# Four parts at once in a spectral-mixing kernel: tables turned by the DMA crossbar, stage-1 evacuations shared anew, a table angle moved, and a drain by groups

## The chip, the cores and the metric

One core of a Trainium2 chip. The metric is the device time in microseconds (us). Most executions of one kernel agree within 0.3%. The kernel before takes 173.03 us (median of 3, 173.02 to 173.04).

The engines carry the profile's names: PE is TensorE (matmuls; PEld its weight loads), DVE is VectorE, ACT is ScalarE, POOL is GpSimd, and SP is SyncE, on whose queue most DMAs are issued. PSUM is the memory into which matmuls write; a result is evacuated when ACT or DVE copies it out. The granted clock is the share of TensorE's full clock that the profile records in a stretch.

## The reference

```python
x = A_x                                            # 1 x 2048 x 512, bf16
W = w_r + 1j * w_i                                 # 2048 x 257
y = irfft2(rfft2(layernorm(x)) * W, s=(2048, 512)).astype(bf16)
h = x + y
r = relu(layernorm(h) @ w1 + b1)                   # 512 -> 1792
out = h + ((r * r) @ w2 + b2)                      # 1792 -> 512
```

The Fourier transform over the 2048 rows is split as 128 x 16, and everything is matmuls with sine and cosine tables. Six stages matter below. Stage 1 transforms along the 128-long axis with a table KF that is folded with LayerNorm's 1/sigma (KFr), and gives Bt. Stage 2 transforms the 512 columns (table GF, result U). Stage 3 finishes the row transform (table EF, results AB and X), and the spectral weights follow on VectorE (mA, mB, Z, M). Stage 4 goes back along the rows (table EI, result T), stage 5 along the columns (table GI, result R), and stage 6 along the other row axis (table KI). LayerNorm and the MLP follow.

## The kernel before

The inverse tables EI and KI are the transposes of EF and KF. The kernel before makes them with TensorE, and copies and negates them on ScalarE and VectorE:

```python
def transposed(o, ks, kf=False):                   # TensorE, into a PSUM tile
    for j, k in enumerate(ks):
        for i in range(2):
            nc.tensor.transpose(o[:, P*(2*j+i):P*(2*j+i)+P], EF[:, k, i, :], ident[:])
    if kf:
        nc.tensor.transpose(o[:, 2*P*len(ks):2*P*len(ks)+P], KF[:, 0:P], ident[:])
def table_i(o, ks):                                # ScalarE
    nc.scalar.copy(EI[:, sl, 0:2, :], o[...])
def table_neg(ks):                                 # VectorE
    nc.vector.tensor_scalar(EI[:, .., 2, :], EI[:, .., 0, :], -1.0, None, ALU.mult)
```

PSUM tiles of the first half come from one pool: four buffers of two banks each. A stage-1 step of two row groups takes one such buffer; a split step takes two, and uses half of each, so that ScalarE empties one and VectorE the other:

```python
ps = tc.alloc_tile_pool(name="ps", bufs=4, space=PSUM)
def mm_tile(name, dt=FP32):
    return ps.tile([P, 4096 // size(dt)], dt, tag="mm", name=name)

def stage1(g0, n=0, split=False, pre=None, cp=nc.scalar.copy):
    if split:
        two = [mm_tile("p1a"), mm_tile("p1b")]
        pts = [pt[:, 0:512] for pt in two]
    else:
        pt = mm_tile("p1"); pts = [pt[:, 0:512], pt[:, 512:1024]]
    ...                                            # 8 matmuls
    if split:
        for t, cph in ((0, nc.scalar.copy), (1, nc.vector.tensor_copy)):
            cph(dst[:, 2*t:2*t+2], pts[t]...)
    else:
        cp(dst, pt[:]...)
...
angles_g(1)                                        # GpSimd: two angle rows, ahead of the power
ln1_rstd(10, 14)                                   # GpSimd: 1/sigma of groups 10 to 13
...
stage1(10, cp=nc.vector.tensor_copy)
# W1, W2, b1, b2 loads issued here
stage1(12)
# GF's last column halved, EF's sines negated (VectorE)
tr08 = stage1(14, split=True, pre=lambda o: transposed(o, (0, 8), True))
```

The drain, between stage 5 and the MLP, with `warm` a run of matmuls on ones whose results nobody reads:

```python
s5(0); s5(1); s5(2, True); s5(3, True)             # stage 5, groups 0 to 3
s5b(0); s5b(1)                                     # R = even + odd, even - odd (VectorE)
s6(0); s6b(0, True); s6(1); s6a(1); s6b(1)         # stage 6, residual, statistics
rstd(0); norm(0)
warm(idle[:], 12)
s5b(2)
transp(0, 0); transp(0, 1)                         # LayerNorm output turned for the MLP
for c in range(5): run(c)                          # the MLP
```

## Time and profile before

The prediction below shows the lines themselves. They boil down to this table, with the starts in us from the start of the span.

| what | before |
|---|---|
| timed median | 173.03 |
| span of the profiled execution | 171.1 |
| busy: PE, VectorE (DVE), ScalarE (ACT) | 92%, 74%, 62% |
| last half of Bt starts on DVE | 19.71 |
| PE's last wait before a stretch without gaps | ends 29.10 |
| stage 5's first matmul | 50.07 |
| MLP's first matmul | 57.13 |

From the MLP's first matmul on nothing changes but for a few copies that the drain now postpones to there, so any gain has to show up in one of the last four rows.

### The profile page before, as it was taken

What the parts mean: (1) busy time and instruction counts of PE and PEld (TensorE: products, weight loads), DVE (VectorE), ACT (ScalarE), POOL (GpSimd) and SP (SyncE); (2) the same over time, 40 slices, a digit from 0 to 9 for tenths busy, and PEclk for the clock granted to TensorE, in tenths of its full rate; (3) what the DMA queues carried; (4) which work ended last, traced back from release to release, by engine and by line L of the source; (5) the groups of instructions that cost most, each with busy time, mean ns of one, the idle gap of its engine ahead of it and who ended that gap; (6) DMA issues with size and microseconds to landing.
All of it is one profiled execution on the core that took longest, in us unless ns stands there. A gap on an engine that the chain in (4) does not pass through costs nothing.

```text
span 171.1 us, 2723 instructions
## 1 busy us (share of the span) xinstructions
PE 158.0 (92%) x982; PEld 93.0 (54%) x997; DVE 125.9 (74%) x294; ACT 106.7 (62%) x188; POOL 36.3 (21%) x63
## 2 busy tenths in 40 slices
PE   3978897999989899899999999999999999999992
PEld 1455665877853675466445444544544454566461
DVE  6998789899957699758997577498667567578321
ACT  3999587998977582288662677254377534478200
POOL 7788800000000002235000135000035200025000
PEclk9999999999999999999999999999999999999999
DMA  5970759910000000010001100001000001010011
GB/s 158 349 261 2 215 168 397 297 35 2 0 0 4 0 0 2 32 35 0 0 21 31 44 0 0 2 31 34 31 31 0 0 31 34 13 48 0 0 59 38
DMA packets 7918, 10.29 MB, mean 60 GB/s; under 512 B 2272, under 2 KB 6368, under 8 KB 7904
## 3 DMA queue, kind: packets, MB, share of 16 engines
q1 hardware_dynamic: 7744, 9.19, 16.6%
q0 software_dynamic: 160, 0.92, 1.8%
q8 instruction: 8, 0.13, 0.3%
q14 instruction: 6, 0.05, 0.1%
HBM read 8.01 MB, written 2.10 MB: 59 GB/s over the span
## 4 chain that ended last, share of the span: by engine, by line
PE 69%; DVE 19%; ACT 6%; issue 3%; POOL 1%; DVEq 0%; POOLq 0%; ACTq 0%
PE ph L688 29%; PE po L721 25%; DVE st L221 4%; PE p L568 3%; PE p L362 3%; PE p L643 2%; ACT U L379 2%; PE po L709 2%; DVE KFr L232 2%; PE p L587 1%; DVE hs L591 1%; DVE mA L437 1%; ACT X L409 1%; DVE mB L437 1%; DVE Z L442 1%
## 5 line engine op out<-in xcount | busy, mean ns | idle before, releaser
L688 PE MATMUL ph<-UT,W 128*128 128x384 bf16 (+2 forms) x278 | 49.8, 336 | 1.5 <-ACT UT L647 1.0
L691 ACT ACTIVATE rl<-ph,b1f 128x384 bf16<-128x384 f32 (+2 forms) x70 | 41.5, 602 | 14.2 <-PE ph L688 11.0
L721 PE MATMUL po<-W,act 128*128 128x512 bf16 x203 | 48.1, 379 | 0.4
L692 DVE TENSOR_TENSOR act<-rl 128x384 bf16<-128x384 bf16 (+2 forms) x70 | 34.2, 514 | 16.2 <-ACT rl L691 15.7
L695 POOL TENSOR_TENSOR hb<-hs,b2b 128x512 f32<-128x512 bf16 x16 | 18.4, 1151 | 102.6 <-DVE act L692 102.6
L688 PEld LDWEIGHTS <-W 128*128 128x128 bf16 x280 | 27.4, 98 | 22.7 <-issue 1.9
L721 PEld LDWEIGHTS <-act 128*128 128x128 bf16 x210 | 20.4, 98 | 21.8
L725 DVE TENSOR_TENSOR ot<-po,hb 128x512 bf16<-128x512 f32 x15 | 10.3, 688 | 9.3 <-PE po L721 8.0
L571 ACT COPY od<-p 128x256 f32<-128x256 f32 x16 | 5.9, 368 | 9.1 <-PE p L568 9.0
L647 ACT COPY UT<-p 128x768 bf16<-128x768 bf16 (+2 forms) x5 | 4.2, 841 | 10.8 <-PE p L643 10.8
L591 DVE SCALAR_TENSOR_TENSOR hs<-p,xs 128x512 bf16<-128x512 f32 x15 | 10.2, 683 | 0.8 <-PE p L587 0.5
L265 PE MATMUL p<-ones 128*128 128x512 bf16 x22 | 7.3, 476 | 2.9 <-POOL ones L152 2.9
L568 PE MATMUL p<-GI,T 128*128 128x256 bf16 x64 | 9.1, 272 | 0.6 <-DVE T L489 0.2
L265 PEld LDWEIGHTS <-ones 128*128 128x128 bf16 x41 | 4.4, 109 | 7.6 <-POOL ones L152 2.9
L602 ACT ACTIVATE junk<-hs 128x512 bf16<-128x512 bf16 x6 | 3.8, 630 | 7.6 <-DVE hs L591 7.6
L362 PE MATMUL p<-GF,Bt 128*128 128x256 bf16 x64 | 8.3, 273 | 0.0
L568 PEld LDWEIGHTS <-T 128*128 128x128 bf16 x64 | 6.2, 97 | 3.9 <-issue 0.9
L250 PE MATMUL p<-KFr,xs 128*128 128x256 bf16 x28 | 6.4, 273 | 2.0 <-DVE KFr L232 2.0
L577 DVE TENSOR_TENSOR R<-p,od 128x256 bf16<-128x256 f32 x16 | 6.6, 414 | 2.1 <-ACT od L571 2.1
L221 DVE BATCH_NORM_STATS2 st<-xs 128x6 f32<-128x512 bf16 x12 | 7.8, 676 | 0.0
L491 ACT CAST T<-p 128x1024 bf16<-128x1024 f32 x7 | 7.2, 1027 | 0.0
L362 PEld LDWEIGHTS <-Bt 128*128 128x128 bf16 x64 | 6.1, 98 | 1.4 <-DVE Bt L257 0.4
(173 smaller groups left out, 228.7 us busy)
## 6 DMA issues: line engine op xcount, KB each, us to landing
W<-in_B_w_dram SPq DMA_DIRECT2D x2, 1792.0 KB, 9.7
out_dram<-ot SPq DMA_DIRECT2D x15, 128.0 KB, 1.8
xs<-in_A_x_dram SPq DMA_DIRECT2D x3, 512.0 KB, 5.6
WB<-in_A_w_r_dram SPq DMA_DIRECT2D x1, 578.2 KB, 5.3
WB<-in_A_w_i_dram SPq DMA_DIRECT2D x1, 578.2 KB, 6.3
xs<-in_A_x_dram SPq DMA_DIRECT2D x2, 256.0 KB, 3.3
b2b<-in_B_b_dram SPq DMA_DIRECT2D x1, 128.0 KB, 8.9
out_dram<-ot SPq DMA_DIRECT2D x2, 64.0 KB, 1.5
```

The source lines that it names most:

```text
L221: nc.vector.bn_stats(st[:], xs[:, g, :])
L265: nc.tensor.matmul(o, lhsT=ones[:, 0:P], rhs=ones[:], start=True, stop=True)
L362: nc.tensor.matmul(puv[:, :, e, :], lhsT=Bt[:, 2 * t + 1 - e, 2 * pr + q, :], rhs=GFv[:, t, :, e, :], start=(t == 0), stop=(t == 1))
L491: nc.scalar.copy(dst, src[0])
L568: nc.tensor.matmul(pe[:, 256 - 256 * e:512 - 256 * e], lhsT=T2[:, lt, g].rearrange("p q s -> p (q s)"), rhs=GI[:, lt, :], start=(r == 0), ...
L591: nc.vector.scalar_tensor_tensor(hs[:, g, :], Ys.pop(g)[:], WSC, xs[:, g, :], ALU.mult, ALU.add)
L688: nc.tensor.matmul(ph[:, 0:n], lhsT=W1[:, d, bass.ts(f, P)], rhs=UT[:, d, 0:n], start=(d == 0), stop=(d == ND - 1))
L691: nc.scalar.activation(rl[:, 0:n], ph[:, 0:n], ACT.Relu, bias=b1f[:, f:f + 1], scale=1.0)
L692: sq = nc.vector.tensor_tensor(act[:, f, 0:n], rl[:, 0:n], rl[:, 0:n], ALU.mult)
L695: add = nc.gpsimd.tensor_tensor(hb[:, g, :], hs[:, g, :], b2b[:], ALU.add)
L721: nc.tensor.matmul(po[:], lhsT=act[:, f, bass.ts(i, P)], rhs=W2[:, f, :], start=(f == 0), stop=(f == NF - 1))
L725: nc.vector.tensor_tensor(ot[:], po[:], hb[:, g, :], ALU.add)
```

## The change

The intent is to take the making of the inverse tables off the three compute engines and give it to the DMA crossbar, to use the room this makes on ScalarE for the stage-1 evacuations, and to shorten the drain by letting group 1's sum and difference come out of matmuls (with a negated table, GIn), so that groups 0 and 1 don't queue on VectorE. The core of the diff, cut:

```diff
-    EF = fwd.tile([P, 9, 3, P], ...)   EI = fwd.tile([P, 9, 3, P], ...)   EN = ...
+    EF = fwd.tile([P, 3, 9, P], ...)   EI = fwd.tile([P, 9, 4, P], ...)
+    GIn = persist.tile([P, 2, 256], BF16, name="GIn")
-    def transposed ... table_i ... table_neg ... first_tables
+    def turned(dst, src):
+        nc.sync.dma_start_transpose(out=dst, in_=...)
@@ stage 1
-    angles_g(1)
-    ln1_rstd(10, 14)
+    nc.gpsimd.tensor_scalar(fiG[:, 512:768], ...)
+    ln1_rstd(10, 14)
+    nc.gpsimd.tensor_scalar(fiG[:, 768:1024], ...)
-    stage1(10, cp=nc.vector.tensor_copy)
-    stage1(12)
+    stage1(10)
+    stage1(12, split=True)
     # GF, EF negation
-    tr08 = stage1(14, split=True, pre=lambda o: transposed(o, (0, 8), True))
+    stage1(14, split=True)
+    turned(EI[:, :, 0, :], EF[:, 0, :, :])         # 9 blocks of sines
+    turned(KI[:].unsqueeze(1), KF[:, 0:P])
+    for k in (0, 8):
+        turned(EI[:, k:k+1, 1, :], EF[:, 1, k, :])
+    turned(EI[:, :, 2, :], EF[:, 2, :, :])         # 9 blocks of negated sines
     ...
+    turned(EI[:, 1:8, 1, :], EF[:, 1, 1:8, :])     # 7 blocks of cosines
+    turned(EI[:, 1:8, 3, :], Cn[:])                # 7 blocks of negated cosines
+    # W1, W2, b1, b2 loads now issued here
@@ spectral part, after pair 5
     sin_of(GI, fiI)
+    nc.scalar.activation(GIn[:], <the even angles of fiI>, ACT.Sin, scale=-SIN_SCALE)
@@ drain
-    s5(0); s5(1); s5(2, True); s5(3, True)
-    s5b(0); s5b(1); s6(0); s6b(0, True); s6(1); s6a(1); s6b(1); rstd(0); norm(0)
-    warm(idle[:], 12)
-    s5b(2); transp(0, 0); transp(0, 1)
+    s5_first(0)        # the odd sum in a bank of its own
+    s5_whole(1)        # 8 matmuls make sum and difference, one ACT copy takes both
+    s5b(0); s6(0); s6(1)
+    rest = [s5(2, True), s5(3, True)]              # their od copies postponed
+    s6a(1); s6b(0, True); s6b(1); ...
+    warm(idle[:], 11)
+    # sqrt, reciprocal, norm, 4 transposes and one copy, group by group
+    for r in rest: r()
+    s5b(2)
```

More of the change, by code (lines that the diff above doesn't have):

```diff
@@ L88 @@
     GF = fwd.tile([P, 2, 512], BF16, name="GF")
-    EF = fwd.tile([P, 9, 3, P], BF16, name="EF")
-    EI = fwd.tile([P, 9, 3, P], BF16, name="EI")
+    EF = fwd.tile([P, 3, 9, P], BF16, name="EF")
+    EI = fwd.tile([P, 9, 4, P], BF16, name="EI")
     ON_PE = (2, 4, 6)
-    Cn = fwd.tile([P, len(ON_PE), P], BF16, name="Cn")
+    Cn = fwd.tile([P, 7, P], BF16, name="Cn")
     NO_M = (5, 6)
-    EN = fwd.tile([P, len(NO_M), 2 * P], BF16, name="EN")
     KFr = fwd.tile([P, G, 256], BF16, name="KFr")
@@ L191 @@
     nc.gpsimd.tensor_scalar(cols[:, 1:2], pF[:, 0:1], 128.0, 16384.0, ALU.mult, ALU.add)
-    def angles_g(t):
-        o = 512 * t
-        for r, q in ((0, QT), (256, HT)):
-            nc.gpsimd.tensor_scalar(fiG[:, o + r:o + r + 256], idxL[:, r:r + 256], cols[:, t:t + 1], float(q),
-                                    ALU.mult, ALU.add)
     def table_e(i):
-        nc.scalar.activation(EF[:, :, i, :], fiE[i][:].bitcast(I16)[:, ::2].rearrange("p (a b) -> p a b", a=9),
+        nc.scalar.activation(EF[:, i, :, :], fiE[i][:].bitcast(I16)[:, ::2].rearrange("p (a b) -> p a b", a=9),
                              ACT.Sin, scale=SIN_SCALE)
@@ L265, in warm @@
             nc.tensor.matmul(o, lhsT=ones[:, 0:P], rhs=ones[:], start=True, stop=True)
-    def transposed(o, ks, kf=False):
-        for j, k in enumerate(ks):
-            for i in range(2):
-                nc.tensor.transpose(o[:, P * (2 * j + i):P * (2 * j + i) + P], EF[:, k, i, :], ident[:])
-        if kf:
-            nc.tensor.transpose(o[:, 2 * P * len(ks):2 * P * len(ks) + P], KF[:, 0:P], ident[:])
-    def table_i(o, ks):
-        n, sl = len(ks), slice(ks[0], ks[-1] + 1, ks[1] - ks[0])
-        nc.scalar.copy(EI[:, sl, 0:2, :], o[:, 0:2 * P * n].rearrange("p (a k b) -> p a k b", a=n, k=2))
-    def table_neg(ks):
-        nc.vector.tensor_scalar(EI[:, ks[0]:ks[-1] + 1, 2, :], EI[:, ks[0]:ks[-1] + 1, 0, :], -1.0, None, ALU.mult)
+    def turned(dst, src):
+        nc.sync.dma_start_transpose(out=dst, in_=src.rearrange("p a b -> p (a b)") if len(src.shape) == 3 else src)
     def angles_c(sl):
@@ L287, in table_c @@
     def table_c(sl):
-        nc.scalar.activation(EF[:, sl, 1, :], fiE[1][:].bitcast(I16)[:, ::2].rearrange("p (a b) -> p a b", a=9)[:, sl],
+        nc.scalar.activation(EF[:, 1, sl, :], fiE[1][:].bitcast(I16)[:, ::2].rearrange("p (a b) -> p a b", a=9)[:, sl],
                              ACT.Sin, scale=SIN_SCALE)
@@ L312 @@
     ln1_fold(6, 10)
-    angles_g(1)
+    nc.gpsimd.tensor_scalar(fiG[:, 512:768], idxL[:, 0:256], cols[:, 1:2], float(QT), ALU.mult, ALU.add)
     ln1_rstd(10, 14)
+    nc.gpsimd.tensor_scalar(fiG[:, 768:1024], idxL[:, 256:512], cols[:, 1:2], float(HT), ALU.mult, ALU.add)
     gathers = [w_reversed(0)]
@@ L326 @@
     ln1_fold(14, 16)
-    stage1(10, cp=nc.vector.tensor_copy)
-    for k, (dst, src) in enumerate(((W1[:], B_w1.rearrange("(c p) f -> p c f", p=P)),
-                                    (W2[:], B_w2.rearrange("(i p) d -> p i d", p=P)),
-                                    (b1b[:], B_b1.rearrange("(i p) -> p i", p=P)),
-                                    (b2b[:], B_b2.unsqueeze(0).to_broadcast([P, D])))):
-        load = nc.sync.dma_start(dst, src)
-        if k == 0:
-            for ga in gathers:
-                after(load, ga, "the rows of W first")
-    stage1(12)
-    nc.vector.tensor_scalar(GF[:, :, 255:256], GF[:, :, 255:256], 0.5, None, ALU.mult)
-    nc.vector.tensor_scalar(EF[:, :, 2, :], EF[:, :, 0, :], -1.0, None, ALU.mult)
-    tr08 = stage1(14, split=True, pre=lambda o: transposed(o, (0, 8), True))
+    stage1(10)
+    stage1(12, split=True)
+    nc.vector.tensor_scalar(GF[:, :, 255:256], GF[:, :, 255:256], 0.5, None, ALU.mult)
+    nc.vector.tensor_scalar(EF[:, 2, :, :], EF[:, 0, :, :], -1.0, None, ALU.mult)
+    stage1(14, split=True)
+    turned(EI[:, :, 0, :], EF[:, 0, :, :])
+    turned(KI[:].unsqueeze(1), KF[:, 0:P])
+    for k in (0, 8):
+        turned(EI[:, k:k + 1, 1, :], EF[:, 1, k, :])
+    turned(EI[:, :, 2, :], EF[:, 2, :, :])
     nc.gpsimd.tensor_scalar(cols[:, 4:5], pF[:, 0:1], 256.0, 128.0, ALU.mult, ALU.add)
@@ L349, in cos_negs @@
     def cos_negs():
-        nc.vector.tensor_scalar(Cn[:], EF[:, ON_PE[0]:ON_PE[-1] + 1:ON_PE[1] - ON_PE[0], 1, :], -1.0, None, ALU.mult)
+        nc.vector.tensor_scalar(Cn[:], EF[:, 1, 1:8, :], -1.0, None, ALU.mult)
+        turned(EI[:, 1:8, 3, :], Cn[:])
     table_c(slice(1, 8))
+    turned(EI[:, 1:8, 1, :], EF[:, 1, 1:8, :])
     GFv = GF[:].rearrange("p t (r e j) -> p t r e j", r=2, e=2)
@@ L387, in stage3 @@
             for u, k1 in ((0, 0), (1, 8)):
-                C, Sp, Sn = EF[:, k1, 1, :], EF[:, k1, 0, :], EF[:, k1, 2, :]
+                C, Sp, Sn = EF[:, 1, k1, :], EF[:, 0, k1, :], EF[:, 2, k1, :]
                 o = pxs[u][:, 0:512]
@@ L395, in stage3 @@
         elif pr in ON_PE:
-            C, Sp, Sn, Cm = EF[:, pr, 1, :], EF[:, pr, 0, :], EF[:, pr, 2, :], Cn[:, ON_PE.index(pr), :]
+            C, Sp, Sn, Cm = EF[:, 1, pr, :], EF[:, 0, pr, :], EF[:, 2, pr, :], Cn[:, pr - 1, :]
             px = mm_tile("p3")
@@ L411, in stage3 @@
             px = mm_tile("p3")
-            C, Sp, Sn = EF[:, pr, 1, :], EF[:, pr, 0, :], EF[:, pr, 2, :]
+            C, Sp, Sn = EF[:, 1, pr, :], EF[:, 0, pr, :], EF[:, 2, pr, :]
             nc.tensor.matmul(px[:, 0:512], lhsT=C, rhs=U[:, 0, :], start=True, stop=False)
@@ L476, in stage4 @@
             if M is None:
-                en = EN[:, NO_M.index(pr), :]
+                en = ei[:, 2 * P:4 * P]
                 mms = [(u, r, ei[:, P:3 * P]) for u in range(2)]
@@ L491, in stage4 @@
             nc.scalar.copy(dst, src[0])
-    def first_tables():
-        nc.vector.tensor_copy(KI[:], tr08[:, 4 * P:5 * P])
-        nc.vector.tensor_scalar(EI[:, 0::8, 2, :], EI[:, 0::8, 0, :], -1.0, None, ALU.mult)
     new_u(0)
@@ L501 @@
     stage2_one(1, 0, nc.scalar.copy)
-    nc.vector.tensor_copy(EI[:, 0::8, 0:2, :], tr08[:, 0:4 * P].rearrange("p (a k b) -> p a k b", a=2, k=2))
     cos_negs()
+    for k, (dst, src) in enumerate(((W1[:], B_w1.rearrange("(c p) f -> p c f", p=P)),
+                                    (W2[:], B_w2.rearrange("(i p) d -> p i d", p=P)),
+                                    (b1b[:], B_b1.rearrange("(i p) -> p i", p=P)),
+                                    (b2b[:], B_b2.unsqueeze(0).to_broadcast([P, D])))):
+        load = nc.sync.dma_start(dst, src)
+        if k == 0:
+            for ga in gathers:
+                after(load, ga, "the rows of W first")
     stage3(0)
@@ L513 @@
             stage2(pr + 3)
-        if pr == 0:
-            tr = mm_tile("ptr", BF16)
-            transposed(tr, (1, 2, 3))
-            table_i(tr, (1, 2, 3))
         if 1 < pr and pr + 2 < 8:
@@ L525 @@
             warm(mm_tile("idle")[:, 0:512], 3)
-        if pr == 3:
-            table_neg((4, 7))
-            nc.vector.tensor_scalar(EN[:].rearrange("p n (k b) -> p n k b", k=2), EI[:, NO_M[0]:NO_M[-1] + 1, 0:2, :],
-                                    -1.0, None, ALU.mult)
         if pr == 0:
-            spectral(0, first_tables)
+            spectral(0)
         elif pr < 8:
             spectral(pr)
-        if pr == 1:
-            table_neg((1, 3))
-            tr = mm_tile("ptr", BF16)
-            transposed(tr, (4, 5, 6, 7))
-            table_i(tr, (4, 5, 6, 7))
         if pr == 5:
             sin_of(GI[:].rearrange("p t c -> p (t c)"), fiI[:])
+            nc.scalar.activation(GIn[:], fiI[:].bitcast(I16)[:, ::2].rearrange("p (t c) -> p t c", t=4)[:, 0::2, :],
+                                 ACT.Sin, scale=-SIN_SCALE)
             nc.gpsimd.tensor_copy(b1f[:], b1b[:])
@@ L569, in s5, with rest, s5_first, s5_whole @@
                                  rhs=GI[:, lt, :], start=(r == 0), stop=(r == 1))
-        od = ffn.tile([P, 256], FP32, tag="od", bufs=4, name="od")
-        nc.scalar.copy(od[:], pe[:, 256:512])
-        Rs[g] = pe, od
+        def rest():
+            od = ffn.tile([P, 256], FP32, tag="od", bufs=4, name="od")
+            nc.scalar.copy(od[:], pe[:, 256:512])
+            Rs[g] = pe, od
+        if ahead:
+            return rest
+        rest()
+    def s5_first(g):
+        two = [bank("p5o", "ph", 3), bank("p5", "pp", 3)]
+        for e in range(2):
+            for r in range(2):
+                nc.tensor.matmul(two[e][:, 0:256], lhsT=T2[:, 2 * r + e, g].rearrange("p q s -> p (q s)"),
+                                 rhs=GI[:, 2 * r + e, :], start=(r == 0), stop=(r == 1))
+        od = ffn.tile([P, 256], FP32, tag="od", bufs=4, name="od")
+        nc.scalar.copy(od[:], two[0][:, 0:256])
+        Rs[g] = two[1], od
+    def s5_whole(g):
+        pe = bank("p5", "pp", 3)
+        for h in range(2):
+            for k, lt in enumerate((1, 3, 0, 2)):
+                nc.tensor.matmul(pe[:, 256 * h:256 * h + 256], lhsT=T2[:, lt, g].rearrange("p q s -> p (q s)"),
+                                 rhs=GIn[:, lt // 2, :] if h and k > 1 else GI[:, lt, :], start=(k == 0), stop=(k == 3))
+        Rs[g] = R = ffn.tile([P, 512], BF16, tag="R", bufs=3, name="R")
+        nc.scalar.copy(R[:], pe[:])
     def s5b(g):
@@ L748, in run @@
                 at += cost
-    s5(0)
-    s5(1)
-    s5(2, True)
-    s5(3, True)
+    u2 = ffn.tile([P, 4, D], BF16, tag="u2", bufs=2, name="u2")
+    UTs[0] = ffn.tile([P, ND, 512], BF16, tag="UT", bufs=2, name="UT")
+    s5_first(0)
+    s5_whole(1)
+    s5b(0)
+    s6(0)
+    s6(1)
+    rest = [s5(2, True), s5(3, True)]
     idle = bank("idle", "ph", 3)
-    s5b(0)
-    s5b(1)
-    s6(0)
+    s6a(1)
     s6b(0, True)
-    s6(1)
-    s6a(1)
     s6b(1)
-    rstd(0)
-    norm(0)
-    warm(idle[:], 12)
+    nc.vector.tensor_scalar(mv2[:, 0, 0:1], mv2[:, 0, 0:1], 1.0 / D, None, ALU.mult)
+    warm(idle[:], 11)
+    for g in range(2):
+        nc.scalar.activation(sd2[:, g:g + 1], mv2[:, g, 1:2], ACT.Sqrt, bias=eps[:], scale=1.0 if g else float(D) ** -3)
+    for g in range(2):
+        nc.vector.reciprocal(rs2[:, g:g + 1], sd2[:, g:g + 1])
+        nc.vector.tensor_scalar(u2[:, g, :], hs[:, g, :], mv2[:, g, 0:1], rs2[:, g:g + 1], ALU.subtract, ALU.mult)
+    for g, cp in ((0, nc.scalar.copy), (1, nc.vector.tensor_copy)):
+        pt = bank("p7", "pp", 3, BF16)
+        for d in range(ND):
+            nc.tensor.transpose(pt[:, P * d:P * d + P], u2[:, g, bass.ts(d, P)], ident[:])
+        cp(UTs[0][:, :, P * g:P * g + P], pt[:, 0:ND * P].rearrange("p (d c) -> p d c", d=ND))
+    for r in rest:
+        r()
     s5b(2)
-    transp(0, 0)
-    transp(0, 1)
     for c in range(5):
```

## The prediction

> **What bounds the kernel now.** I first read the page's totals and its chain that ended last. The span is 171.1 us and the timed median 173.03 us; I carry differences in the span straight over to the time.
>
> ```profile
> span 171.1 us, 2723 instructions
> PE 158.0 (92%) x982; PEld 93.0 (54%) x997; DVE 125.9 (74%) x294; ACT 106.7 (62%) x188; POOL 36.3 (21%) x63
> PE 69%; DVE 19%; ACT 6%; issue 3%; POOL 1%; DVEq 0%; POOLq 0%; ACTq 0%
> ```
>
> TensorE (PE) carries 69% of the chain, VectorE (DVE) 19%. In the chain in order of time, everything from 57.13 us on is the MLP (L688, L721), a stream of matmuls with under 3 us of waits. The diff leaves that part alone, so the change can win only in the 57 us ahead of it, and what it wins there should move the end one for one. I read those 57 us as timelines, engine by engine, in three stretches.
>
> Stretch 1, the end of stage 1, DVE alone:
>
> ```profile
> 15.06 0.48 DVE L232 TENSOR_SCALAR KFr<-KF,rs 128x256 bf16<-128x256 bf16 x2 [0.41 <-POOL rs L228]
> ...
> 17.41 0.48 DVE L232 TENSOR_SCALAR KFr<-KF,rs 128x256 bf16<-128x256 bf16 x2 [0.46 <-POOL rs L323]
> 17.81 1.22 DVE L260 CAST Bt<-p 128x1024 bf16<-128x1024 f32 x1
> 18.94 0.40 DVE L338 TENSOR_SCALAR GF<-GF 128x2 bf16<-128x2 bf16 x1
> 19.01 0.67 DVE L339 TENSOR_SCALAR EF<-EF 128x1152 bf16<-128x1152 bf16 x1
> 19.71 0.69 DVE L257 CAST Bt<-p1b 128x512 bf16<-128x512 f32 x1
> ```
>
> DVE waits for GpSimd's rstd, then does a whole evacuation of Bt, and so reaches the last half of Bt only at 19.71; it ends at 20.40, and stage 2's first matmuls that read it load at 20.46. ScalarE (ACT) is idle 0.84 us just before (17.1 to 17.96).
>
> Stretch 2, the spectral part, PE:
>
> ```profile
> 29.10 0.38 PE L413 MATMUL p<-U,EF 128*128 128x512 bf16 x1 [0.81 <-ACT U L379]
> ...
> 31.73 0.61 PE L270 MATMUL ptr<-ident,EF 128*128 128x128 bf16 x8
> ...
> 32.18 1.04 PE L362 MATMUL p<-GF,Bt 128*128 128x256 bf16 x8
> ...
> 48.15 0.39 PE L464 MATMUL p4a<-EI,M 128*128 128x256 bf16 x2 [0.35 <-DVE M L452]
> ```
>
> Between these two bracketed waits PE issues without a gap: a 512-column matmul every 0.22 us, a 256-column one every 0.11, a transpose every 0.055. From 29.1 to 47.7 us PE is busy 18.4 of 18.6 us, ACT 17.5 and DVE 17.3. PE sets the pace and the others are close behind. The end of this stretch on ACT:
>
> ```profile
> 44.70 1.09 ACT L124 ACTIVATE GI<-fiI 128x1024 bf16<-128x1024 int16 x1
> 45.66 1.03 ACT L491 CAST T<-p 128x1024 bf16<-128x1024 f32 x1
> 46.71 1.28 ACT L543 ACT_TABLE_LOAD   x1
> 48.00 0.29 ACT L543 ACTIVATE junk<-eps 128x1 f32<-128x1 f32 x1
> 48.21 0.99 ACT L491 CAST T<-p 128x1024 bf16<-128x1024 f32 x1
> 49.10 0.59 ACT L488 CAST T<-p4a 128x512 bf16<-128x512 f32 x1
> ```
>
> ACT is without slack here; T's last half on DVE ends at 49.92.
>
> Stretch 3, the drain from stage 5 to the MLP:
>
> ```profile
> 50.75 1.64 ACT L571 COPY od<-p 128x256 f32<-128x256 f32 x4 [1.06 <-PE p L568]
> 52.70 0.39 PE L587 MATMUL p<-R,KI 128*128 128x512 bf16 x1 [0.27 <-DVE R L578]
> 52.92 2.75 PE L265 MATMUL idle<-ones 128*128 128x512 bf16 x12
> 56.49 0.59 ACT L647 COPY UT<-p 128x512 bf16<-128x512 bf16 x1 [1.40 <-PE p L643]
> 57.13 1.47 PE L688 MATMUL ph<-UT,W 128*128 128x256 bf16 x12 [0.45 <-ACT UT L647]
> ```
>
> This is latency: stage 5 starts at 50.07, the MLP at 57.13, 7.06 us of copies, R sums, LayerNorm and transposes for two groups.
>
> **What the Trainium skill says.** "DMA: Bandwidth & Descriptors", section "DMA Transpose (X-bar)", allows such a transpose only for 2-byte types, into SBUF, from the Sync or Scalar queues; all of these are bf16 and issued from SP. Section "Rules for kernel authors" there says that a transpose next to ordinary DMAs needs nothing, and "Latency and other measured facts" gives 261 GB/s for non-contiguous DMA transposes. No DMA transpose is in the trace before, so nothing there confirms it. "TensorE: Matmul & The Clock Gate", "Part 4: PE-mode transpose", says that a PE transpose lands in PSUM and needs a copy after: the trace agrees, with 1.84 us of ACT copies (L277, 0.81 and 1.03) for 14 transposes, at 219 ns each where the page has about 275.
>
> **The change part by part.**
>
> *Tables by DMA.* 9 + 1 + 2 + 9 + 7 + 7 = 35 blocks of 128 by 128 bf16, 32 KB each, 1.15 MB: at the page's 261 GB/s some 4.4 us of transfer (estimate), plus some 2 us each of start and landing (the trace's 128 KB output stores land in 1.8). Their sources are ready at 5 (EF sines, KF), 14.4 (two cosines), 19 to 20 (negated sines), 20 (cosines) and 22 us (Cn); first use is stage 4 at 30.8. So I expect them wholly hidden. W1 and W2 now queue behind them: issued at 22.03 before, perhaps 23 to 26 now, landing in 9.7, needed at 57. Hidden too, with 20 us to spare.
>
> What goes away: on PE 5 transposes in stage 1 and 14 later; on ACT 1.84 us; on DVE the EI copy 0.41, KI 0.22, EI's negations 0.22 + 0.29 + 0.29, EN 0.28, sum 1.7, plus the 0.66 us wait for EI at 33.3. But how much of this lies on the path? Up to 29.10 the path runs U, stage 3, X on ACT, U, stage 3, with none of it in it. From there PE is the bound, and only its 8 transposes from 31.73 to 32.18 leave its stream: 0.45 us. DVE, freed of more, would then wait for AB of pair 5, which waits for PE: before it was in time to 0.17 us. So stretch 2 wins 0.45 us on PE and DVE.
>
> Against it stands the new GIn on ACT (512 columns; 256 of this function took 0.43 and 896 took 0.96, so about 0.64, of which about 0.54 is until the next can start). ACT's T copy of pair 4 moves from 43.79 to 43.34, GI to 44.25, GIn to 45.20, T of pair 5 from 45.66 to 45.74, the table load, T of pair 6 and the last half to 49.17, end 49.76. DVE's half ends at about 49.48. Stage 5 now waits for ACT: 49.76 against 49.92, a gain of 0.16 us instead of 0.45. I take 0.17.
>
> *Stage 1.* The second half of the stage's angles now comes after rstd on GpSimd, so rstd ends 0.53 us earlier (14.5) and the fold at 15.06 goes to about 14.7. The last folds wait for a power on GpSimd that sits behind the gather's issue, so they gain only 0.2: 17.21. Then DVE evacuates half a tile (0.6) in place of a whole one (1.13): 0.53. Sum 0.73; the last half of Bt would start at 18.98 and end at 19.67. ACT has room: whole stage 10 at 17.0, the halves of 12 and 14 at 17.9 and 18.4. PSUM buffers turn in time (stage 14's second half needs stage 10's, free at 18.03). Everything up to 29.10 moves with it.
>
> *Drain*, counted from stage 5's first matmul. Group 0's odd sum is two matmuls alone in a bank, so its copy starts at 0.46 instead of 0.68; R of group 0 ends at 1.68 (before 1.90). Group 1 needs no DVE sum: 8 matmuls end at 1.5, ACT's 512-column copy (0.59) ends at 2.15, its stage 6 starts at 2.22 where before it stood at 2.63. Then hs 0.43 later, statistics to 4.3, sqrt to 4.6, u of group 0 done at 4.9 and of group 1 at 5.45. If PE were free, transposes and copies would let the MLP start at 6.36. But stage 5 of groups 2 and 3 (8 matmuls, 0.87) now lies between stage 6 and the 11 warming matmuls (11 by 0.213, 2.34), so PE is occupied until 2.43 + 0.87 + 2.34 = 5.65. Transposes then, 0.44 for all eight, copies to 6.67, MLP at about 6.7: gain 0.36 us (0.70 without the warming ones in the way). The postponed od copies (0.37 each) and R of group 2 fall into 6.0 to 7.4, ahead of stage 6 of group 2, which is 1.2 us into the MLP.
>
> Sum: 0.73 + 0.17 + 0.36 = 1.26 us, so 173.03 - 1.26 = 171.8 us.
>
> **The rivals.**
>
> 1. *The crossbar is slow, or holds up SP.* For: nothing in the trace measures it, and SP waits in program order, so W loads stand behind Cn. If stage 4 waited for its table, each us would be a us; W late beyond 57 the same. It takes 8 us in the first case, 20 in the second. That would make 173 to 178.
> 2. *The whole of the removed work counts.* ACT and DVE are each busy over 93% of stretch 2, and their 1.8 and 1.7 us less would pass through if they, not PE, set the pace; with the unblocked drain that is 0.73 + 1.7 + 0.7 = 3.1, 169.9 us. Against: PE's gapless issue, and the ACT tail with GIn.
> 3. *GIn and the warming matmuls eat it.* If GIn costs its whole 0.64 and the drain's gain is nil, stage 1 alone stays: 172.3 us.
>
> **Range and chances.** The stage-1 and spectral terms rest on measured durations; each may be off by 0.3, the drain by 0.4, the DMA has a tail on the slow side. I give 170.8 to 172.9 us. Faster by over 2% would need 169.6, more than rival 2's whole sum: 0.03. Slower by over 2% needs rival 1 at its worst: 0.03. Within 2%: 0.94.
>
> **What would show it.** Right: stage 4 never waits on a DMA; Bt's last half ends near 19.7; PE streams without a gap from about 28.4; ACT's T copies late by GIn, so that stage 5 follows ACT, not DVE; the drain's PE goes from warming straight to transposes; the MLP starts near 55.9 and takes the same 114 us. Wrong: a DMA among PE's releasers, a new gap in PE between 28 and 47, an MLP with stalls for hb, bias or R, or a drain that is still above 7 us.

## More of the kernel before

One more line of before is needed later. It is PE's timeline near the end of stage 1; the columns are start, busy time, engine, line, operation, output and inputs, count, and in brackets the idle time before it with what ended it:

```profile
19.08 0.27 PE L250 MATMUL p1b<-KFr,xs 128*128 128x256 bf16 x1 [0.43 <-DVE Bt L260]
```

The second half of stage 14 waited until DVE had emptied stage 10's buffer (at 19.03). It cost nothing in that kernel, because DVE was not free to take this half before 19.71.

## The result, and the profile after

The changed kernel takes 172.59 us (median of 4, 172.54 to 172.67), beside 173.03 (median of 4, 173.02 to 173.32) of the kernel before in the same rounds. The ratio is 0.9971, with a 95% interval of 0.9954 to 0.9988. Ratios here are the mean time of one kernel's fast runs over that of the other's of the same rounds, so not quite the ratio of the medians. The gain is about 0.44 us (0.3%), where 1.26 were foreseen. The time is inside the range, but two thirds of the gain are missing.

| start of | before | after | gain in this stretch | foreseen |
|---|---|---|---|---|
| last half of Bt on DVE | 19.71 | 19.73 | -0.02 | 0.73 |
| PE's stretch without gaps | 29.10 | 29.12 | 0 | 0 |
| stage 5 | 50.07 | 49.83 | 0.26 | 0.17 |
| MLP | 57.13 | 56.66 | 0.23 | 0.36 |
| DVE's last output sum | 167.99 | 167.53 | -0.01 | 0 |

The table by stretches says at once where to look: stage 1. First, what went well. The page's first line, and the timeline of the Sync engine's queue (SPq; the busy time here is how long the issue holds the queue):

```profile
span 170.8 us, 2709 instructions
```

```profile
7.29 3.65 SPq L262 DMA_TRANSPOSE EI<-EF  x1
...
14.75 8.99 SPq L262 DMA_TRANSPOSE EI<-EF  x4
23.83 1.25 SPq L262 DMA_TRANSPOSE EI<-Cn  x1
25.18 1.09 SPq L485 DMA_DIRECT2D W<-in_B_w_dram  x2
```

The transposes hold the queue far longer than a load does (a plain load just before them took 0.43). The line of x4 merges four of them and a gap of 1.9 us before the third; taken singly, the seven of this run took 1.1 to 1.4 us each, but for the first (3.65) and the one at 20.75 (2.99). They push the loads of W1 and W2 from 22.03 to 25.18. The last one, of Cn, lands 3.1 us after its issue, so at about 27, and the first stage 4 starts at 30.85. W lands 10.3 us after its issue, at about 36, and the MLP needs it at 56.66. No DMA stands among the releasers of PE. Now PE at the points that answer to those of before:

```profile
18.66 0.27 PE L244 MATMUL p1a<-KFr,xs 128*128 128x256 bf16 x1 [0.78 <-DVE Bt L251]
...
29.12 0.38 PE L395 MATMUL p<-U,EF 128*128 128x512 bf16 x1 [1.15 <-ACT U L361]
...
49.83 0.39 PE L558 MATMUL p5o<-GI,T 128*128 128x256 bf16 x2 [0.42 <-ACT T L470]
```

The first line is the news: stage 14's first half waits 0.78 us for DVE's copy of Bt. DVE at the same place:

```profile
14.62 0.71 DVE L226 TENSOR_SCALAR KFr<-KF,rs 128x256 bf16<-128x256 bf16 x2
...
17.91 0.69 DVE L251 CAST Bt<-p1b 128x512 bf16<-128x512 f32 x1
...
18.59 0.45 DVE L314 TENSOR_SCALAR EF<-EF 128x1152 bf16<-128x1152 bf16 x1
19.73 0.69 DVE L251 CAST Bt<-p1b 128x512 bf16<-128x512 f32 x1 [0.69 <-PE p1b L246]
```

The fold came 0.44 us earlier (15.06 before) and the evacuation became half as long, as planned. DVE was through with everything at about 19.04. It then stood idle for 0.69, because PE had not made the last half, and that because PE had waited for the copy at 17.91. All that was won on DVE was waited away. The end of the spectral part on ACT:

```profile
45.23 0.65 ACT L513 ACTIVATE GIn<-fiI 128x512 bf16<-128x512 int16 x1
...
49.19 0.59 ACT L470 CAST T<-p4a 128x512 bf16<-128x512 f32 x1
```

ACT is late by GIn and ends at 49.78, and stage 5 waits for ACT, no longer for DVE. And the drain:

```profile
51.99 0.38 PE L587 MATMUL p<-R,KI 128*128 128x512 bf16 x1
...
53.29 2.32 PE L259 MATMUL idle<-ones 128*128 128x512 bf16 x10
...
54.70 0.41 DVE L769 TENSOR_SCALAR u<-hs,mv,rs 128x512 bf16<-128x512 bf16 x1
55.45 0.61 PE L773 MATMUL p<-ident,u 128*128 128x128 bf16 x8
...
56.66 1.47 PE L688 MATMUL ph<-UT,W 128*128 128x256 bf16 x12 [0.61 <-DVE UT L774]
```

The second group's u is ready at 55.11, the first group's long before (54.59), but PE runs through its queue of warming matmuls and goes straight from them into the eight transposes at 55.45.

### The profile page after: what moved, and what is told of

The parts are those of the page before. It is cut to its first block, busy times and chain, and to the rows that moved or that the text cites. A ratio compares the mean times of both kernels' runs of the same rounds, so it can differ in the third digit from the quotient of the medians.

```text
span 170.8 us, 2709 instructions
## 1 busy us (share of the span) xinstructions
PE 157.6 (92%) x967; PEld 92.4 (54%) x981; DVE 123.6 (72%) x287; ACT 106.3 (62%) x188; POOL 36.7 (22%) x63
## 4 chain that ended last, share of the span: by engine, by line
PE 72%; DVE 16%; ACT 5%; issue 2%; POOL 2%; DVEq 0%; POOLq 0%; ACTq 0%
PE ph L688 29%; PE po L721 25%; DVE st L215 3%; PE p L542 3%; PE p L344 3%; ACT U L361 2%; PE po L709 2%; PE p L643 2%; PE p L587 1%; PE idle L259 1%; POOL rs L222 1%; DVE KFr L226 1%; DVE mA L419 1%; ACT X L391 1%; DVE mB L419 1%
## 5 line engine op out<-in xcount | busy, mean ns | idle before, releaser
L725 DVE TENSOR_TENSOR ot<-po,hb 128x512 bf16<-128x512 f32 x15 | 10.3, 688 | 9.3 <-PE po L721 8.0
L591 DVE SCALAR_TENSOR_TENSOR hs<-p,xs 128x512 bf16<-128x512 f32 x15 | 10.3, 684 | 1.2 <-PE p L587 0.9
L259 PE MATMUL p<-ones 128*128 128x512 bf16 x22 | 8.1, 516 | 2.9 <-POOL ones L152 2.9
L546 ACT COPY od<-p 128x256 f32<-128x256 f32 x14 | 5.1, 370 | 7.9 <-PE p L542 7.9
L647 ACT COPY UT<-p 128x768 bf16<-128x768 bf16 (+1 forms) x4 | 3.6, 906 | 9.4 <-PE p L643 9.4
L542 PE MATMUL p<-GI,T 128*128 128x256 bf16 x56 | 8.2, 272 | 0.4 <-DVE hs L591 0.2
L542 PEld LDWEIGHTS <-T 128*128 128x128 bf16 x56 | 5.4, 97 | 3.5 <-issue 1.2
L605 DVE BATCH_NORM_STATS2 st<-hs 128x6 f32<-128x512 bf16 x9 | 6.3, 695 | 0.3
## 6 DMA issues: line engine op xcount, KB each, us to landing
W<-in_B_w_dram SPq DMA_DIRECT2D x2, 1792.0 KB, 10.3
```

Of the source, the lines that this page charges most:

```text
L259: nc.tensor.matmul(o, lhsT=ones[:, 0:P], rhs=ones[:], start=True, stop=True)
L542: nc.tensor.matmul(pe[:, 256 - 256 * e:512 - 256 * e], lhsT=T2[:, lt, g].rearrange("p q s -> p (q s)"), rhs=GI[:, lt, :], start=(r == 0), ...
L591: nc.vector.scalar_tensor_tensor(hs[:, g, :], Ys.pop(g)[:], WSC, xs[:, g, :], ALU.mult, ALU.add)
L725: nc.vector.tensor_tensor(ot[:], po[:], hb[:, g, :], ALU.add)
```

## The experiments

My theory after the result was this. *Buffers*: stage 1's 0.73 us was lost because stage 14 got a PSUM buffer that DVE had yet to empty; in the built program its first half and stage 12's second half have the same two banks. (Building the kernel again confirms it: of the eight banks, 0 to 7, stages 8 and 10 have the pairs that begin at 0 and 6, the halves of stage 12 those at 4 and 2, the halves of stage 14 those at 2 and 0.) *GIn* costs some 0.2 us at stage 5. *Warming* costs some 0.3 to 0.5 us in the drain. The rivals: the crossbar's transfers, in flight during stage 1, slow it; or the tables' removal is worth nothing and the 0.24 has another source. Eleven kernels were run, in three calls (no run e5); each call had its own runs of the kernel before (medians 173.02, 173.16 and 173.03). Where medians are set side by side, the ratios are the check.

One nuisance goes through all of them. In some executions the rows of x land some 0.1 to 1.0 us later in stage 1, and everything after moves by as much. The kernel before has it too (172.89 to 173.49). Where a profile fell into such an execution I say so, and compare within the profile or by the medians.

| kernel | median us (lowest to highest) | ratio to before |
|---|---|---|
| changed kernel | 172.59 (172.54 to 172.67) | 0.9971 [0.9954, 0.9988] |
| e1_one_tile | 172.90 (172.51 to 173.46) | 0.9992 [0.9974, 1.001] |
| e2_gin_early | 172.67 (172.33 to 173.05) | 0.9978 [0.9962, 0.9993] |
| e3_warm6 | 172.06 (172.04 to 172.13) | 0.9943 [0.9931, 0.9956] |
| e4_tables_only | 172.63 (172.53 to 173.04) | 0.9982 [0.997, 0.9994] |
| e6_old_drain | 172.79 (172.75 to 173.75) | 0.9981 [0.9969, 0.9993] |
| e7_half_banks | 172.03 (171.92 to 172.32) | 0.9938 [0.9925, 0.995] |
| e8_all_three | 171.24 (171.23 to 171.34) | 0.9893 [0.9878, 0.9907] |
| e9_late_turn | 172.73 (172.51 to 172.86) | 0.9975 [0.9962, 0.9987] |
| e10_banks_old_sharing | 172.73 (172.64 to 173.32) | 0.998 [0.9967, 0.9994] |
| e11_warm3 | 171.36 (171.26 to 171.55) | 0.9904 [0.9889, 0.9919] |
| e12_warm0 | 172.31 (171.26 to 172.85) | 0.9935 [0.9903, 0.9966] |

### e1: both halves of a split step in one tile

```diff
         if split:
-            two = [mm_tile("p1a"), mm_tile("p1b")]
-            pts = [pt[:, 0:512] for pt in two]
+            pt = mm_tile("p1s")
+            two = [pt, pt]
+            pts = [pt[:, 0:512], pt[:, 512:1024]]
```

A split step then takes one buffer instead of two, and stage 14 need not wait for stage 12's.

> The changed kernel, but stage 12 and stage 14 each put their two halves into the two banks of one PSUM buffer instead of two half-used buffers, so stage 14 no longer gets the buffer that DVE has just emptied for stage 12. Buffer theory (stage 1 won nothing because PE waited 0.78 us for DVE to empty stage 12's second half): the wait before stage 14's first matmul goes, its matmuls start near 17.95 instead of 18.66, the last half of Bt starts on DVE near 19.06 instead of 19.73, everything after moves up by 0.65 us, and the time is 171.9 to 172.0 against 172.6. Rival (the first crossbar transposes delay the x rows by 0.25 us and ACT by 0.36, and that is what ate the gain): Bt's last half stays near 19.7 and the time stays at 172.5 to 172.6.

This missed. PE's wait is gone (stage 14 starts loading at 17.80), but no time was won: 172.90. DVE shows why:

```profile
18.86 0.69 DVE L252 CAST Bt<-p1s 128x512 bf16<-128x512 f32 x1 [0.92 <-ACT Bt L252]
```

Two engines now read one tile, and the program as built orders them: DVE's half starts only when ACT's is done. The last half of Bt comes at 20.15, stage 5 at 50.23. One wait was exchanged for another, so this says nothing yet about what the buffers cost. It took e7 to separate the two.

### e2: GIn early

```diff
             stage2(pr + 3)
+        if pr == 0:
+            <the activation that makes GIn>
...
             sin_of(GI[:]..., fiI[:])
-            <the activation that makes GIn>
```

> The changed kernel, but GIn is made early, right behind the U copy of pair 3, where ACT stands idle for 1.1 us, instead of behind GI. Theory (GIn delays ACT's T copies, so that stage 5 waits for ACT): T of pair 5 starts near 45.2 instead of 45.75, the last half on ACT ends near 49.3, stage 5 waits for DVE's half and starts near 49.6 instead of 49.83; the time falls by 0.2 us to 172.4. Rival (the tail of ACT is set by PE and the table load, not by GIn): stage 5 still starts at 49.8 and the time stays at 172.6.

The median did not move (172.67). The fastest run, 172.33, is 0.21 below the fastest of the changed kernel. The profile fell in an execution with late rows: the last half of Bt starts at 20.17, 0.44 later than in the changed kernel. Yet stage 5 is only 0.25 later:

```profile
50.08 0.38 PE L559 MATMUL p5o<-GI,T 128*128 128x256 bf16 x2 [0.23 <-DVE T L471]
```

So, counted from stage 1, it is 0.19 earlier, and it waits for DVE again. GIn at the end of ACT's chain costs 0.19 us, by the profile; the timing alone would not have shown it. The trace of e4, which has no GIn, agrees: stage 5 starts there at 49.62, 0.21 before the changed kernel.

### e3: six warming matmuls instead of eleven

```diff
-    warm(idle[:], 11)
+    warm(idle[:], 6)
```

> The changed kernel with 6 instead of 11 warming matmuls in the drain. Theory (PE was still warming when u of group 0 was ready at 54.6): group 0's transposes start near 54.7 and group 1's near 55.2 instead of all at 55.5, the MLP starts near 56.1 instead of 56.66, and the time falls by 0.5 us to 172.1. Rival (the gap left on PE lowers its pace for the first MLP matmuls, or the copies and not the transposes are what ends last): the MLP starts within 0.15 us of 56.66, or its matmuls are slower at first, and the time is 172.5 or more.

```profile
54.63 0.92 PE L773 MATMUL p<-ident,u 128*128 128x128 bf16 x8
...
56.16 1.03 PE L688 MATMUL ph<-UT,W 128*128 128x256 bf16 x8 [0.61 <-DVE UT L774]
```

Stage 5 is at 49.81, and the transposes of the first group start when its u is ready, at 54.63. The MLP starts 6.35 us after stage 5, where the changed kernel had 6.83. The time is 172.06, half a us less, with a spread of 0.09. The granted clock stayed at 0.997 to 1.0. So five of the eleven were a pure loss.

### e4: the crossbar tables alone

The kernel before with the tables turned by the crossbar: its own order of angles, its own sharing of stage 1, its own drain, no GIn. The edit is the change's diff without the hunks "angles", "stage 1 (sharing)", "GIn" and "drain".

> The kernel before with the crossbar tables alone: old order of angles and sharing in stage 1, old drain, no GIn. Theory (of the removed work only PE's 8 transposes inside its gapless stream count, 0.45 us): stage 5 starts near 49.6 against 50.07 in the kernel before, and the time is 172.6. Rival A (the removed ACT and DVE work counts in full): stage 5 starts near 48.3, time 171.3. Rival B (the crossbar traffic costs something in stage 1 or the loads): time at or above 172.9, with a DMA among the releasers of PE, ACT or DVE.

```profile
49.62 1.91 PE L540 MATMUL p<-GI,T 128*128 128x256 bf16 x16 [0.23 <-DVE T L471]
```

Stage 5 is at 49.62 instead of 50.07: 0.45 us, as much as the eight transposes of 0.055 that left PE's stream. (That it is these and nothing else is read from the sizes: no run takes out the transposes alone.) The last half of Bt is at 19.71, as before, and the MLP is at 56.67. The median is 172.63, so the tables alone give 0.4 us by the medians (0.3 by the ratio), nearly as much as the whole change. The idea that all the removed work of ACT and DVE (1.8 and 1.7 us) would count is refuted.

### e6: the changed kernel with the old drain

The drain of the kernel before put back, GIn still computed but not read.

> The changed kernel with the drain of the kernel before (GIn is still made). Theory (the new drain won 0.23 us as its traces say): stage 5 starts at 49.83 as in the changed kernel, the MLP 7.06 later near 56.9, time 172.8. Rival (the new drain wins nothing, since its postponed copies are paid in the first MLP chunk): time 172.6.

172.79, against 172.59 with the new drain: by the medians it is worth 0.2 us, and the two ranges do not overlap. The profile fell in an execution with late rows (0.97 later at the last half of Bt), but within it the drain from stage 5 (50.80) to the MLP (57.86) is 7.06 us, as long as before to the hundredth. The new one takes 6.83.

### e7: own banks for the split steps

```diff
-    ps = tc.alloc_tile_pool(name="ps", bufs=4, space=PSUM)
+    ps1 = tc.alloc_tile_pool(name="ps1", bufs=2, space=PSUM)     # two whole buffers
...
-            two = [mm_tile("p1a"), mm_tile("p1b")]
+            two = [ps1.tile([P, 512], FP32, tag="half", bufs=4, name=k) for k in ("p1a", "p1b")]
...
     stage1(14, split=True)
+    warm(ps1.tile([P, 512], FP32, tag="half", bufs=4, name="pw")[:], 3)   # moved from stage 2
+    ps1.release()
+    cur[0] = ps = tc.alloc_tile_pool(name="ps", bufs=4, space=PSUM)
```

The eight banks become two whole buffers and four single banks during stage 1, so each of the four halves has a bank that no one has to empty first, and each tile has one reader.

> The changed kernel, but in stage 1 the PSUM is cut into two whole buffers and four single banks, so that each half of stages 12 and 14 has a bank of its own (the first try, one buffer for both halves, put a new wait of DVE for ACT in place of PE's wait for DVE). Three warming matmuls are kept, into one of these banks. Buffer theory: stage 14's matmuls start near 17.95 instead of 18.66, without a wait for DVE's evacuation; the last half of Bt starts on DVE near 19.05 instead of 19.73; U of pair 0 starts on DVE near 20.45 instead of 21.01; everything after moves up by 0.55 us; time 172.05. Rival (the x rows and ACT, late by 0.36 us, set the end of Bt): ACT's last half ends later than DVE's, near 19.9, and the time stays above 172.4.

```profile
18.00 0.68 DVE L252 CAST Bt<-p1b 128x512 bf16<-128x512 f32 x1
...
19.03 0.68 DVE L252 CAST Bt<-p1b 128x512 bf16<-128x512 f32 x1
```

```profile
49.35 0.39 PE L562 MATMUL p5o<-GI,T 128*128 128x256 bf16 x2 [0.42 <-ACT T L474]
```

Stage 14 loads at 17.94, DVE goes through without a wait, and the last half starts at 19.03 instead of 19.73. Of these 0.70 us 0.46 reach U of pair 0 (20.55 after 21.01), and 0.48 stage 5. The rest stays on PE: here all twelve first matmuls of stage 2 start only after DVE's copy (at 19.86), where in the changed kernel one had its weights loaded before it (at 19.96, the copy ending at 20.42). Probably the new pool gets its banks only then; no run tested that. The median is 172.03, 0.56 below the changed kernel (0.57 by the ratios). ACT's last half of Bt ends at 19.52, before DVE's at 19.71, so the rival of the recorded expectation, a late ACT, does not set the end of Bt. Buffers were the cause. The rows were some 0.13 late in this profile (the last folds at 17.60, not 17.47); e8, with the same banks and rows on time, gives the cleaner number: PE's stretch without gaps starts at 28.51 instead of 29.12, so 0.6 us are what the prediction's stage-1 step would have brought with these banks.

### e8: own banks, GIn early and six warming matmuls together

e7, e2 and e3 in one kernel.

> Own banks for the halves, GIn made early, and 6 warming matmuls in the drain, all together. If the three losses are separate: 0.55 + 0.2 + 0.5 = 1.25 us off the changed kernel's 172.6, so 171.3 to 171.4, faster than both. If they overlap (for instance stage 5 then waits for PE or DVE in another way): 171.6 or more.

```profile
55.36 1.47 PE L693 MATMUL ph<-UT,W 128*128 128x256 bf16 x12 [0.61 <-DVE UT L779]
```

171.24 us, four runs within 0.11, 1.9 us below the kernel before of its call (1.07% by the ratio): the fastest kernel. Stage 5 is at 49.03, the MLP at 55.36, the span 169.4. The parts add up: 0.56 (e7) + 0.19 (e2, from the profile) + 0.53 (e3) is 1.28, and 172.59 - 171.24 is 1.35. By the ratios it is 0.57 + 0.19 + 0.48, so 1.24, against 1.35.

### e9: the first transposes issued later

```diff
     stage1(14, split=True)
-    turned(EI[:, :, 0, :], EF[:, 0, :, :])
-    turned(KI[:].unsqueeze(1), KF[:, 0:P])
     for k in (0, 8):
         turned(EI[:, k:k + 1, 1, :], EF[:, 1, k, :])
+    turned(EI[:, :, 0, :], EF[:, 0, :, :])
+    turned(KI[:].unsqueeze(1), KF[:, 0:P])
```

No crossbar transfer is issued before 14.7 us, so none lies beside the loads of x.

> The changed kernel, but the crossbar transposes of the sines and of KF, which go out at 7.3 us while the last x rows are still landing, are issued after those of the two cosine tables, from 14.7 us on. Theory (the crossbar takes nothing from the path): ACT's wait of 0.25 us for the x rows at 8.4 shrinks or goes, Bt's last half still starts on DVE near 19.7, and the time stays at 172.6; stage 4 still never waits for a DMA. Rival (the crossbar traffic delays stage 1 through the x rows): time 172.2 to 172.4.

172.73, no faster than the changed kernel. Stage 14 waits 0.78 for DVE's copy all the same. The profiled execution had late rows again, with no transpose in flight. So the first transposes are not the reason for stage 1's loss, and rows come late without them too. In e9 ACT's wait for rows at 8.4, 0.25 us in the changed kernel, is gone, but an earlier one, of 0.18 before 5.67, is there. In e4 the wait at 8.4 was 0.47, and in e3, e7 and e8, with the same early transpose, the profile marks none, so nothing ties it to the transposes; that they add to it now and then is not excluded. In e4 it cost nothing, since the last half of Bt started at 19.71 as before.

### e10: own banks with the old sharing

e4 with e7's banks: is it the banks alone?

> The tables alone (old order of angles, old sharing of stage 1, old drain), but with banks of their own for stage 14's halves. Theory (own banks and the new sharing win only together, because with the old sharing DVE itself reaches the last half of Bt no earlier than 19.7): stage 14's second half no longer waits on PE at 19.08, its matmuls are done near 18.8, but DVE still starts that copy at 19.6 to 19.7 and the time is the 172.6 of the tables alone. Rival (the buffers alone are worth the 0.55 us and the new sharing nothing): the copy starts near 19.1 to 19.2 and the time is 172.1.

172.73, against 172.63 of e4: nothing won. In this profile (rows about 0.4 late) DVE is busy with its whole evacuation of stage 10, GF and EF until 20.08, and its last half starts at 20.23 after a wait of only 0.15. So the banks pay only together with the half evacuation, up to that 0.15. It is not a clean test, because stage 12 has only two whole buffers here and waits 0.82 for ACT to empty stage 8's.

### e11 and e12: three and no warming matmuls

```diff
-    warm(idle[:], 6)
+    warm(idle[:], 3)      # e11
+                          # e12: the line is gone
```

Both are e8 otherwise.

> The three mendings together with 3 warming matmuls in the drain instead of 6. Theory: with 6 the transposes already follow u, so fewer win nothing: MLP 6.33 us after stage 5 as with 6, time 171.2 to 171.3. Rival (PE loses pace after a longer idle): the first MLP matmuls are slower and the time is 171.5 or more.

> As the one with 3, but with no warming matmuls at all in the drain, so that PE idles some 1.5 us. Theory: if warming is not needed over so short a gap, 171.2 to 171.3; if it is, the first matmuls of the MLP, or the transposes, are slower than 0.11 us apart and the time is 171.5 or more.

Three give 171.36 and the MLP at 55.37 where six had it at 55.36: the transposes wait for u, so fewer warmings free nothing more. The clock stayed at 0.997 to 1.0 with three too. None gives 172.31, one run in four as fast as e8 (171.26) and three not (172.00, 172.61, 172.85). The mean granted clock is 0.99 in the two slowest of these and 0.999 in the one of 172.00, so that one was slow mainly for another reason, perhaps late rows. The profile is of the slowest (its rows some 0.3 late). PE around its gap in it, and windows of the first MLP matmuls, first of e12, then of e8; the columns of these are length, busy time and count of PE, PEld, DVE, ACT and POOL, granted TensorE clock, share of the DMA engines and GB/s:

```profile
54.17 0.92 PE L777 MATMUL p<-ident,u 128*128 128x128 bf16 x8 [1.41 <-DVE u L773]
55.70 2.72 PE L693 MATMUL ph<-UT,W 128*128 128x256 bf16 x12 [0.61 <-DVE UT L778]
```

```profile
55.00:57.00 2.00, 1.39 (x9) 0.96 (x8) 1.13 (x3) 0.93 (x4) 0.00 (x0) 0.62 0.03 8
57.00:60.00 3.00, 3.00 (x20) 2.18 (x19) 1.62 (x6) 1.76 (x5) 0.00 (x0) 0.68 0.00 0
```

```profile
55.00:57.00 2.00, 1.64 (x15) 1.40 (x16) 1.27 (x5) 1.35 (x5) 0.00 (x0) 1.00 0.03 8
```

Without warming the granted clock falls to 0.62 and 0.68 in this execution, and the first twelve MLP matmuls take 2.72 us instead of 1.47. So some warming is needed, and six, or three, kept the clock as well as eleven in every run made.

## Why the prediction was wrong, step by step

**Tables by DMA, "wholly hidden": right.** PE waited for no transpose and, in the MLP, not for W (result; e9 and e4 agree). The rival of a slow crossbar fell.

**Spectral part, 0.17 us: right in mechanism, 0.24 measured** (50.07 to 49.83). PE's stream lost 0.45, the gain of e4, and GIn gave back about 0.2, seen in the profiles of e2 and e4. The 0.07 us more than foreseen are the hand-over to PE, which the prediction took as equal: stage 5 had started 0.15 after DVE's copy (49.92 to 50.07) and now starts 0.05 after ACT's (49.78 to 49.83). The forecast of ACT's tail held to 0.03 us at each step: GIn at 45.20 (measured 45.23), T of pair 5 at 45.74 (45.75), the end at 49.76 (49.78).

**Stage 1, 0.73 us: wrong, 0 measured. This step failed.** The sentence that failed is "PSUM buffers turn in time (stage 14's second half needs stage 10's, free at 18.03)". I had assumed that the four buffers go round in order. The built program gave stage 14's first half the two banks of stage 12's second half, which DVE empties only from 17.91 to 18.60. PE waited 0.78, and DVE then waited 0.69 for PE. The first half of stage 14 was not in the prediction's list at all; its second half, in the event, had stage 8's banks and not stage 10's. Of the other terms two held: the fold was at 14.62 (foreseen about 14.7) and the evacuation took half the time. One failed: the last folds came at 17.47 instead of 17.21, no earlier than before (17.41), because the gather's issue ended 0.25 us later than before and stood in the way of the power on GpSimd. And one gain was not foreseen: GF and EF took DVE 0.43 us between them (18.60 to 19.03 in e7) where they had taken 0.77. So with own banks and rows on time (e8) the last half starts at 18.89, 0.82 us earlier than before, and that this is near the foreseen 0.73 is luck: the unforeseen 0.34 stands in for the missing 0.2. e7 gives the four halves their banks and gets 0.56 us of the 0.73. The profile of before held the warning: the bracket at 19.08, stage 14 waiting for DVE's evacuation of a buffer. I read it as harmless, which it was there, and did not ask what it would do once DVE came 0.7 us earlier.

**Drain, 0.36 us: right in mechanism, 0.23 measured.** PE went from warming into the transposes as foreseen, and the copies ended at 6.68 us after stage 5 (foreseen 6.67). The term too small was the last: from the end of the copy to the first MLP matmul I had put 0.03 us, and it took 0.15. It is the same hand-over: in the kernel before, the last copy that the MLP waited for was ACT's (57.08 to 57.13, 0.05 us), and now it is DVE's (56.51 to 56.66). The note that without warming in the way the MLP could start at 6.36 was met by e3 at 6.35, in part by luck: u of group 1 was ready at 5.28 instead of 5.45, and the rest took as much longer.

**Sum.** 0 + 0.24 + 0.23 = 0.47 us by the profile, and 0.44 by the medians. The missing 0.8 us are 0.73 of stage 1 and 0.13 of the drain, less 0.07 of the spectral part. Rival 3 (GIn and warming eat it, stage 1 alone stays) came nearer with 172.3, but for the opposite reason: stage 1 is what was lost.

**What stays open.** Why some executions get their x rows later. What own banks would bring to the old sharing without e10's shortage of whole buffers. Why EF's negation took 0.45 us in the changed kernel and in e7 but 0.68 in e1 and 0.64 in e10 with the same layout. Here the traces give a strong hint: in all four profiles where it took 0.63 to 0.68 (the kernel before, e1, e4, e10) GpSimd's index row or angle rows of GI ran beside it, and in the nine where it took 0.45 only a one-column operation of GpSimd did, itself at 0.34 to 0.39 us instead of 0.19. Cn's negation behaves alike (0.64 to 0.66 us in e7, e8, e11 and e12 beside the angle rows, 0.38 or 0.39 after them in the other runs that have it in this shape). No run varied this alone.

## What to carry to other kernels

When a change makes an engine come to an evacuation earlier, work out for each PSUM buffer who empties it last and when, from the built program and not from an assumed rotation; a harmless bracket of such a wait in the old trace is the place to start. Work taken off several engines is worth what leaves the stream of the one that sets the pace (here 0.45 us of some 2 us), and each addition to the next one in line, like GIn, is to be put where that engine is idle. Warming matmuls stand in PE's program order, ahead of what follows: give them as many as fit into the real idle time, and test fewer, but not none.

## What the Trainium skill lacked or had wrong

- "DMA: Bandwidth & Descriptors", section "Latency and other measured facts", gives 261 GB/s for a non-contiguous DMA transpose, but no trn2 figure for how long one holds the queue that issues it, or for small ones (only cycles of unnamed earlier generations beside trn3). Here a transpose held the Sync queue 1.1 us (1 block of 32 KB) to 3.65 us (9 blocks), and not by size alone: those 9 blocks went out beside the loads of x and w, and held it 1.37 when e9 issued them at 17.3; 7 blocks took 1.25 and 2.99. A plain load held it 0.43. The last 7 blocks landed 3.1 us after issue, which is 74 GB/s with the start included (229,376 bytes in 3.1 us). At the page's bandwidth they would take 0.9 us (an estimate), so for transposes of this size something other than that bandwidth is most of the time; here the slack hid it.
- "TensorE: Matmul & The Clock Gate", section "Why this matters for your kernels", asks for no PE-idle gap of over some 3 us. In e12 PE was idle only 1.4 us before the transposes, but from 52.76 to 55.70, 2.9 us, it ran nothing but transposes, and in two of four runs the mean granted clock was 0.99; in the profiled one of them it fell to 0.62 over two us. This agrees with the same page's remark in "Part 4: PE-mode transpose" that transposes don't count as busy, and the rule would be safer if it said so. Six matmuls (1.46 us) in the gap were enough in e3 and e8, and three in e11.
- "PSUM — Partial Sum Buffer", section "PSUM bank collisions raise a hardware error", says that two engines on different banks run clean. It does not say that a program as built may order two engines that read different banks of one tile: 0.92 us in e1, none with separate tiles in e7. And no page says that the buffer a tile gets is not simply the next in rotation: 0.78 us of PE and 0.69 of DVE here.
